# Decode attention and an MLP on one core: the projection's weights on every fourth partition, larger last pieces, and another order at the start

## Chip, cores and metric

One core of one Trainium2 chip runs the whole program in one launch. The metric is device time in microseconds; "median of the runs" is over separate timed runs without the profiler, and a profiled execution is one further run whose records are read here. The engines are PE (matrix multiply, with its weight loads listed as PEld), DVE (vector), ACT (scalar functions), POOL (general), and SP, which here only issues transfers. The transfers of SP's and ACT's queues run on 16 DMA engines.

## The reference, cut to what matters

```python
def _A_ref(x, k_cache, v_cache, wq, wo):          # B=2, Sq=1, D=1024, H=32, Sk=16384, Dh=128, bf16
    q = (x @ wq).reshape(B, Sq, H, Dh).transpose(0, 2, 1, 3)
    scores = einsum("bhqd,bhkd->bhqk", q, k_cache) * (Dh ** -0.5)
    p = softmax(scores)
    o = einsum("bhqk,bhkd->bhqd", p, v_cache)
    return o.transpose(0, 2, 1, 3).reshape(B, Sq, H * Dh) @ wo

def _B_ref(x, w1, w2, w3, w4):                    # F=3584
    h = gelu(layernorm(x) @ w1)
    hs = (quarters of h, shifted along S and padded with zeros) @ w2
    x1 = x + hs
    return x1 + gelu(layernorm(x1) @ w3) @ w4

g = sigmoid((x * gate_w).sum(-1))
out = g * A + (1 - g) * B
```

Each of the two caches is 2 x 32 x 16384 x 128 bf16 values, 256 MiB; K and V together are nearly all of the 572.53 MB that the program reads. With S = 1 every shifted quarter of h is zero, so the product with w2 is one with zeros; the kernel computes it with the zero tile `shT`.

## The kernel before, in words

**Units.** The attention is done in 32 units: 16 head pairs i, and in each the two batch rows s = 0 and 1. A unit's K is 8 MiB, held as 64 KB on each of the 128 partitions, and its V likewise. The buffer `mem` has five cells of 32 KB per partition. K of s = 0 lies in cells 0 and 1, K of s = 1 in cells 1 and 2, V in cells 3 and 4. As the two Ks share a cell, a K may be loaded once the unit before has transposed the first four of its eight chunks, those in the shared cell (semaphore `tr3`). A V may be loaded once the V before has been used (`pvd`).

**One unit in the loop** (L875 to L884). POOL spreads the queries (`pool_unit`, L610). DVE transposes K chunk by chunk into the two buffers `kt` (`dve_scores`, L631); PE multiplies each chunk, 8 matmuls (`pe_scores`, L654). DVE transposes the scores and takes the maximum m (L638, L640). `softmax` (L663): ACT makes Dm, a diagonal matrix of m; PE spreads it (R); ACT takes the exponent into `pt` with its sums. `pe_pv` (L711) multiplies the V of the unit *before by one head pair* with its `pt`, 64 matmuls into `oacc`, and `dve_pv_end` (L772) adds up the rows into `red`. PE then brings the result into rows (`ot`, L717), and DVE copies it as bf16 to `OT` (L782). After s = 1, `pe_project` (L727) multiplies OT with wo's 256 rows of that head pair and adds to `arow` in PSUM. `total` (L684) takes R's minimum as the exponent's bias `nb` on DVE, sums on PE and inverts on DVE. Each engine goes through its own instructions in order and waits on semaphores, so an order written in the source is the order on each engine.

**SP's queue** in the loop (L868 to L874): wait for `tr3`, load K; wait for `pvd`, load the V of the head pair before; for s = 0 also wait for `wod` (the last projection is done) and load wo: 512 KB as 128 partitions with two rows of 2 KB each, 4 KB in one run. All transfers of the loop are in this one queue, each waiting instruction in front of those after it.

**The start.** SP loads wq into cells 3 and 4, w1 and w2 into cell 2, the first K; then, as cells come free, w3, the second unit's K (L803), w4 (L817) and, in the loop's first iteration, its K (L869) and V. The MLP is done between the first two units: the first layer norm and w1, w2; then the first half of unit 0's chunks; the second layer norm; `x1row` = x + hs on the few rows that hold data (L805 to L813, four DVE operations on two partitions each); the second half; w3's product; unit 0's softmax and `total`; the transpose of w3's product into the scratch `tsc` (L823) and its GELU; unit 1's chunks, w4's product, its softmax and `total`; then `brow` = (x1 + h2)(1 - g), L841 to L856.

**The end.** The V of the last head pair: s = 0 whole into cells 0 and 1 (L894), s = 1 in nine pieces of 32 or 16 rows (a row is one 128-wide position of each partition; 32 of them are 8 KB). The first three pieces go through `pv_moving` as in the loop (L939), the others one row at a time straight into the last accumulation (L952), so that each is used as it lands. Then the last two heads' wo rows, in a tile of their own (`wo_l`), the last projection (L963), the sum with `brow` (L970) and the stores.

`Line` (L21) is a helper that derives waits from names read and written; `ln.wait` makes an engine wait for stamps.

Of the kernel before, what the change touches and what calls it, by code (L numbers as in the profile page):

```python
# [88 lines left out]
def kernel(  # L89
# [36 lines left out]
    FQ = F // Q4  # L126
    HQ = H // Q4
    assert NCK == 8 and NG <= QP and FC * QP == FQ and KC * QP == NQ

# [14 lines left out]
    kt = [sb([P, CT * Dh // 2], FP32, f"kt{k}") for k in range(2)]  # L144
    wo_t = sb([P, 2, D], BF16, "wo")
    wo_l = sb([P, 2, D], BF16, "wo_last")
    st = sb([P, GT, QP], FP32, "st")
    Dm = sb([P, P], FP32, "Dm")
    tsc = sb([P, HQ * Dh], FP32, "tsc")
    xin = sb([P, B, KC], BF16, "xin")  # L150
    xrow = sb([P, NQ], BF16, "xrow")
    gwT = sb([P, KC], BF16, "gwT")
# [22 lines left out]
    h2T = sb([P, FC, B], BF16, "h2T")  # L175
    x1row = sb([P, NQ], FP32, "x1row")
    brow = sb([P, NQ], FP32, "brow")
# [9 lines left out]
    part = sb([P, Dh], FP32, "part")  # L187
    red = sb([P, 2, Dh], FP32, "red")
    OT = sb([P, 2, B], BF16, "OT")
    OTl = sb([P, 2, B], BF16, "OT_last")  # L190
    out_row = sb([P, NQ], BF16, "out_row")

    sps = [psum.tile([P, GT * QP], FP32, name=f"S{k}") for k in range(2)]
# [15 lines left out]
    v_rows = A_v_cache.rearrange("b (g t) s d -> b g (t s d)", t=2)  # L209
    wo_rows = A_wo.rearrange("(g p r) n -> g (p r n)", p=P, r=2)  # L210

# [7 lines left out]
    def wo_source(hp):  # L219
        flat = wo_rows[hp : hp + 1, :] if isinstance(hp, int) else wo_rows[bass.ds(hp, 1), :]  # L220
        return flat.rearrange("o (p x) -> (o p) x", p=P)

# [13 lines left out]
    with tc.tile_critical(no_gpsimd_drain=True):  # L236
# [10 lines left out]
        ln.dma("ACT", xin[:], A_x.rearrange("b s (p r) -> p (b s) r", p=P), "l_x", writes=["xin"])  # L247
        ln.dma("ACT", gwT[:], gate_w.rearrange("(p r) -> p r", p=P), "l_gw", writes=["gwT"])
        for b in range(B):
            ln.dma(  # L250
                "ACT", xrow[b : b + QP * (Q4 - 1) + 1 : QP, :],
                A_x[b, 0].rearrange("(k n) -> k n", k=Q4), f"l_xr{b}", writes=[f"xrow{b}"],
            )
# [12 lines left out]
        for k in range(2):  # L266
            ln.op("POOL", lambda k=k: POOL.memset(pts[k][:], 0.0), writes=[f"pt{k}"])

        for k in range(2):
            ln.op("DVE", lambda k=k: DVE.memset(oacc[k], 0.0), writes=[f"oacc{k}"])  # L270
# [4 lines left out]
        ln.op("DVE", lambda: DVE.memset(shT[:], 0.0), writes=["shT"])  # L275
        ln.op("DVE", lambda: DVE.memset(brow[:], 0.0), writes=["brow"])
        ln.op("DVE", lambda: DVE.memset(hm2[:], 0.0), writes=["hm2"])
# [384 lines left out]

        def softmax(u):  # L663
            s = u.s
            wait(PE, "dm", u.after(1))
            PE.matmul(R_ps[:, 0:P], lhsT=ones_f[:], rhs=Dm[:], start=True, stop=True).then_inc(S("rr"), 1)  # L666
            wait(ACT, "mx", u.after(1))
            ACT.activation(out=Dm[:], in_=ident_s[:], func=ACTF.Copy, scale=m_t[:, 0:1]).then_inc(S("dm"), 1)  # L668
            wait(ACT, "nbd", u.after(1))
            if not u.first:  # L670
                wait(ACT, "pvd", u.after(0))
            for e in range(2):
                rows = slice(e * HALF, (e + 1) * HALF)
                ins = ACT.activation(  # L674
                    out=pts[s][rows, :, e, :].rearrange("p (m a) k -> p a k m", a=GT // 4),
                    in_=st[rows, :, 0:NG].rearrange("p (a k) m -> p a k m", k=4),
                    func=ACTF.Exp,
                    bias=nb_t[rows],
                    scale=scale,
                    accum_out=rs_t[rows],  # L680
                )
            ins.then_inc(S("ex"), 1)

        def total(u):  # L684
            s = u.s
            wait(DVE, "rr", u.after(1))
            for e in range(2):
                rows = slice(e * HALF, (e + 1) * HALF)
                ins = DVE.tensor_reduce(out=nb_t[rows], in_=R_ps[rows, rows], axis=AX.X, op=ALU.min)  # L689
            ins.then_inc(S("nbd"), 1)  # L690
            wait(PE, "ex", u.after(1))
            PE.matmul(tot_ps[:, 0:1], lhsT=lmat[:], rhs=rs_t[:], start=True, stop=True).then_inc(S("tt"), 1)  # L692
            wait(DVE, "tt", u.after(1))
            DVE.reciprocal(out=rinv[s][:], in_=tot_ps[:, 0:1]).then_inc(S("rcp"), 1)  # L694

# [15 lines left out]
        def pe_pv(u):  # L711
# [3 lines left out]
            wait(PE, "rd", u.after(-1))  # L715
            for r in range(2):
                ins = PE.matmul(  # L717
                    ot_ps[:, 2 * r : 2 * r + 2],
                    lhsT=red[:].rearrange("p e d -> p (e d)")[:, r : 2 * Dh : 2],
                    rhs=hsel[:],  # L720
                    start=True,
                    stop=True,
                    skip_group_check=True,
                )
            ins.then_inc(S("otd"), 1)

        def pe_project(u):  # L727
            wait(PE, "wol", u.v_landed)
            wait(PE, "OTd", u.after(-1))
            for r in range(2):  # L730
                for k in range(Q4):
# [40 lines left out]
        def dve_pv_end(u):  # L772
# [4 lines left out]
            dve_rows(s, maskr[s], u.after(-1)).then_inc(S("rd"), 1)  # L777
            wait(DVE, "otd", u.after(-1))
            wait(DVE, "wod", u.i)
            for e in range(2):  # L780
                rows = slice(e * HALF, (e + 1) * HALF)
                ins = DVE.tensor_copy(  # L782
                    out=OT[rows, :, s],
                    in_=ot_ps[rows, 0:4].rearrange("p (r e) -> p e r", e=2)[:, e],
                )
            ins.then_inc(S("OTd"), 1)

# [16 lines left out]
        layernorm_T(x1T[:], xn2T[:], "ln2", "x1T", "xn2T")  # L804
        for g in range(Q4):  # L805
            rows = slice(QP * g, QP * g + B)
            ln.op(
                "DVE",
                lambda rows=rows: DVE.tensor_tensor(  # L809
                    out=x1row[rows, :], in0=ot_ps[rows, :], in1=xrow[rows, :], op=ALU.add  # L810
                ),
                reads=["ot", "xrow0", "xrow1"], writes=["x1row"],
            )  # L813
        dve_scores(u0, NCK // 2)
# [3 lines left out]
        pe_scores(u0, NCK - 1)  # L818
        softmax(u0)
        total(u0)  # L820
        ln.op(
# [7 lines left out]
        gelu_T(columns(FC), h2T[:], FC, "g2", "h2T")  # L829

        pool_unit(u1)
        dve_scores(u1)
        pe_scores(u1, 0, NCK - 1)
        linear(h2T, w4_v, FC, D, "h2T", "c3", [ot_ps[:]], ["ot"])
        pe_scores(u1, NCK - 1)
        softmax(u1)
        total(u1)
        ln.wait("PE", [ln.writer["ot"]])
        PE.sem_inc(S("pvd"), 1)
        PE.sem_inc(S("wod"), 1)  # L840
        for g in range(Q4):  # L841
            rows = slice(QP * g, QP * g + B)
            ln.op(
                "DVE",
                lambda rows=rows: DVE.tensor_tensor(
                    out=brow[rows, :], in0=ot_ps[rows, :], in1=x1row[rows, :], op=ALU.add
                ),
                reads=["ot", "x1row"], writes=["brow"],
            )
        ln.op(  # L850
# [4 lines left out]
            reads=["brow", "omgrow"], writes=["brow"],  # L855
        )  # L856

        with nc.Fori(1, HP) as i:
# [5 lines left out]
            for s in range(2):  # L864
# [7 lines left out]
                if s == 0:  # L872
                    wait(SP, "wod", i)
                    SP.dma_start(out=wo_t[:].rearrange("p r n -> p (r n)"), in_=wo_source(i - 1)).then_inc(S("wol"), 16)  # L874
            for u in units:  # L875
                pool_unit(u)
                dve_scores(u)
                pe_scores(u)
                softmax(u)
                pe_pv(u)  # L880
                dve_pv_end(u)
                if u.s == 1:
                    pe_project(u)
                total(u)  # L884

        landed = [f"l_{x}" for x in ("wq", "w1", "w2", "x", "gw", "xr0", "xr1", "w3", "w4")]
        landed += [f"l_v31_{n}" for n in range(3)]

        def landing(n):
            return 32 if n < 9 else 16  # L890

        PIECES = [32] * 7 + [16] * 2
        wait(SP, "tr3", 2 * HP)
# [3 lines left out]
        for n, size in enumerate(PIECES):  # L897
# [4 lines left out]
            at += size  # L902
        wo_heads = A_wo.rearrange("(h d) n -> d h n", d=Dh)
        for e in range(2):
            SP.dma_start(out=wo_l[:, e, :], in_=wo_heads[:, H - 2 + e, :]).then_inc(S(landed[len(PIECES) + 1 + e]), 16)  # L905

# [32 lines left out]
        for n in range(3):  # L939
            wait(PE, landed[n + 1], landing(n + 1))  # L940
            ins = pv_moving(V, 1, n * 8, (n + 1) * 8, moving // 4)
        ins.then_inc(S("pvd"), 1)
# [66 lines left out]
```

## Time and profile before

| | us |
|---|---|
| runs | 1335.42, 1335.53, 1336.2; median 1335.53 |
| profiled execution: its time | 1336.33 |
| profiled execution: span, first to last instruction | 1334.6 |
| PE busy | 748.9 (56%), 4920 matmuls |
| DVE busy | 710.5 (53%), 712 instructions |
| ACT busy | 104.6 (8%) |
| POOL busy | 12.4 (1%) |
| mean granted PE clock | 0.808 |
| read from HBM | 572.53 MB, 429 GB/s over the span |
| transposes of K (L631) | 256 of 2.28 us, 570.7 |
| score matmuls (L654) | 2048, 548.9 |

The page divides the span into 40 slices and shows how busy each engine and the DMA engines were in them; it lists the costliest groups of instructions with what they waited for; and it follows the chain of work that ended last back through what released each step. For each issue of a transfer the trace has the time from issue to landing, when its semaphore is complete. A transfer's time to landing includes what was queued before it. An idle engine costs nothing while something else sets the end.

### The profile page before, as it was taken

How to read it: one execution, taken by the hardware profiler on the slowest of the kernel's cores; microseconds unless marked ns; L12 is line 12 of the kernel's file. 1: busy time of each engine (PE TensorE's matmuls, PEld its weight loads, DVE VectorE, ACT ScalarE, POOL GpSimd, SP SyncE). 2: the span in 40 equal slices, each digit the busy share in tenths (PEclk: the TensorE clock that was granted, in tenths of full speed). 3: DMA queues.
4: the chain of work that ended last, by engine and by line, in shares of the span. 5: the costliest groups of instructions: out<-in, count | busy, mean ns of one | idle time of the engine just before them, and what ended most of it. 6: DMA issues, size and time to landing. Idle time of an engine off the chain costs nothing.

```text
span 1334.6 us, 11800 instructions
## 1 busy us (share of the span) xinstructions
PE 748.9 (56%) x4920; PEld 302.2 (23%) x4920; DVE 710.5 (53%) x712; ACT 104.6 (8%) x164; POOL 12.4 (1%) x44
## 2 busy tenths in 40 slices
PE   0655666554566555466654546655455665555664
PEld 0222222222222222222222212222222222222222
DVE  1465565654556654456565445655444656545561
ACT  0010000000000000000000000000000000000000
POOL 0000000000000000000000000000000000000000
PEclk9778887777888777788777788877778877777886
DMA  9999999999999999999999999999999999999997
GB/s 409 437 419 425 431 433 432 430 438 430 434 432 434 432 432 438 426 438 430 434 432 434 436 428 438 428 436 431 434 438 428 436 428 438 424 441 436 430 436 317
DMA packets 13993, 572.68 MB, mean 429 GB/s; under 512 B 1936, under 2 KB 1952, under 8 KB 4384
## 3 DMA queue, kind: packets, MB, share of 16 engines
q1 hardware_dynamic: 13544, 572.53, 99.5%
q8 instruction: 8, 0.13, 0.0%
q10 hardware_dynamic: 440, 0.01, 0.0%
q14 instruction: 1, 0.01, 0.0%
HBM read 572.53 MB, written 0.00 MB: 429 GB/s over the span
## 4 chain that ended last, share of the span: by engine, by line
DMA 65%; DVE 16%; PE 12%; issue 5%; SPq 1%; POOL 0%; ACT 0%; POOLq 0%; ACTq 0%
DMA mem<-in_A_k_cache_dram 64%; DVE kt L631 15%; PE S L654 11%; DMA wo_last<-in_A_wo_dram 2%; SPq L898 1%; PE oacc L699 0%; PE oacc L510 0%; ACT pt L674 0%; SPq L905 0%; SPq L869 0%; DVE x1row L809 0%; DVE st L638 0%; POOL ln_rstd L450 0%; POOL qw L265 0%; DVE tsc L823 0%
## 5 line engine op out<-in xcount | busy, mean ns | idle before, releaser
L654 PE MATMUL S<-kt,qw 128*128 128x512 bf16 x2048 | 548.9, 418 | 306.8 <-DVE kt L631 306.7
L631 DVE STREAM_TRANSPOSE kt<-mem 128x2048 f32<-128x2048 f32 x256 | 570.7, 2283 | 208.0 <-DMA mem<-in_A_k_cache_dram 154.6
L654 PEld LDWEIGHTS S<-kt,qw 128*128 128x128 bf16 x2048 | 196.3, 104 | 645.7 <-issue 338.9
L699 PE MATMUL oacc<-mem,pt 128*8 128x512 bf16 x2008 | 115.9, 384 | 4.0 <-DMA mem<-in_A_v_cache_dram 4.0
L674 ACT ACTIVATE pt<-st,nb 64x256 bf16<-64x256 f32 x64 | 89.7, 1401 | 226.0 <-DVE nb L689 225.5
L747 DVE TENSOR_SCALAR part<-oacc,maskr 128x128 f32<-128x128 f32 x31 | 10.9, 351 | 143.0 <-PE oacc L699 143.0
L668 ACT ACTIVATE Dm<-ident_s,m 128x128 f32<-128x128 f32 x32 | 12.8, 401 | 921.2 <-DVE m L640 921.2
L692 PE MATMUL tot<-rs,lmat 128*128 128x1 f32 x64 | 18.7, 362 | 105.3 <-ACT pt L674 105.3
L694 DVE RECIPROCAL rinv<-tot 128x1 f32<-128x1 f32 x32 | 5.4, 168 | 113.1 <-PE tot L692 113.1
L699 PEld LDWEIGHTS oacc<-mem,pt 128*8 128x8 bf16 x2008 | 46.2, 87 | 61.3 <-DMA mem<-in_A_v_cache_dram 4.1
L638 DVE STREAM_TRANSPOSE st<-S 128x512 f32<-128x512 f32 x32 | 22.9, 717 | 69.8 <-PE S L654 69.8
L717 PE MATMUL ot<-hsel,red 128*128 128x2 f32 x120 | 19.0, 263 | 54.7 <-DVE red L753 54.7
L666 PE MATMUL R<-Dm,ones_f 128*128 128x128 f32 x64 | 15.6, 326 | 54.4 <-ACT Dm L668 54.4
L692 PEld LDWEIGHTS tot<-rs,lmat 128*128 128x128 f32 x64 | 16.0, 311 | 112.3 <-ACT pt L674 112.3
L717 PEld LDWEIGHTS ot<-hsel,red 128*128 128x128 f32 x120 | 16.4, 196 | 69.8 <-DVE red L753 69.8
L674 ACT ACTIVATION_READ_ACCUMULATOR pt<-st,nb 64x1 f32 x64 | 30.6, 478 | 0.0
L666 PEld LDWEIGHTS R<-Dm,ones_f 128*128 128x128 f32 x64 | 9.5, 188 | 70.2 <-ACT Dm L668 70.2
L753 DVE SCALAR_TENSOR_TENSOR part<-oacc,maskr,part 128x128 f32<-128x128 f32 x62 | 21.7, 351 | 2.2
L782 DVE CAST OT<-ot 64x2 bf16<-64x2 f32 x60 | 9.6, 160 | 22.2 <-PE ot L717 21.8
L344 PE MATMUL tot<-zp,ones_f 128*128 128x2 f32 x2 | 0.6, 364 | 33.7 <-DVE zp L366 33.7
L615 POOL TENSOR_TENSOR qw<-qd,mask 128x16 bf16<-128x16 f32 (+1 forms) x32 | 8.4, 263 | 1138.6 <-PE S L654 1138.6
L689 DVE TENSOR_REDUCE nb<-R 64x1 f32<-64x64 f32 x64 | 14.2, 222 | 3.4 <-PE R L666 2.1
(104 smaller groups left out, 116.0 us busy)
## 6 DMA issues: line engine op xcount, KB each, us to landing
mem<-in_B_w_dram SPq DMA_DIRECT2D x2, 7168.0 KB, 27.6
wo<-in_A_wo_dram SPq DMA_DIRECT2D x15, 512.0 KB, 28.5
mem<-in_A_v_cache_dram SPq DMA_DIRECT2D x7, 1024.0 KB, 18.4
mem<-in_B_w_dram SPq DMA_DIRECT2D x2, 2048.0 KB, 29.3
mem<-in_A_v_cache_dram SPq DMA_DIRECT2D x2, 512.0 KB, 27.7
mem<-in_A_k_cache_dram SPq DMA_DIRECT2D x32, 28.3
wo_last<-in_A_wo_dram SPq DMA_DIRECT2D x2, 256.0 KB, 21.6
mem<-in_A_v_cache_dram SPq DMA_DIRECT2D x31, 30.9
```

Of the source, the lines that this page charges most:

```text
L631: DVE.transpose(out=kt[n % 2][:], in_=k_view(s)[:, c * CT : (c + 1) * CT, :].rearrange("p j d -> p (j d)").bitcast(FP32),).then_inc(S(f"tr ...
L638: DVE.transpose(out=st[:].rearrange("p j r -> p (j r)"), in_=sps[s][:]).then_inc(S("stT"), 1)
L654: ins = PE.matmul(sps[s][:].rearrange("p (j k) -> p j k", k=QP), lhsT=qw[s][:, v, NG - 1 - m : NG - 1 - m + P], rhs=ktb[:, half * GT : (ha ...
L666: PE.matmul(R_ps[:, 0:P], lhsT=ones_f[:], rhs=Dm[:], start=True, stop=True).then_inc(S("rr"), 1)
L668: ACT.activation(out=Dm[:], in_=ident_s[:], func=ACTF.Copy, scale=m_t[:, 0:1]).then_inc(S("dm"), 1)
L674: ins = ACT.activation(out=pts[s][rows, :, e, :].rearrange("p (m a) k -> p a k m", a=GT // 4), in_=st[rows, :, 0:NG].rearrange("p (a k) m ...
L689: ins = DVE.tensor_reduce(out=nb_t[rows], in_=R_ps[rows, rows], axis=AX.X, op=ALU.min)
L692: PE.matmul(tot_ps[:, 0:1], lhsT=lmat[:], rhs=rs_t[:], start=True, stop=True).then_inc(S("tt"), 1)
L699: ins = PE.matmul(oacc[s][QP * q : QP * q + 8, :], lhsT=pts[s][:, g].rearrange("p h k -> p (h k)"), rhs=V[:, 4 * g : 4 * g + 4, :].rearran ...
L717: ins = PE.matmul(ot_ps[:, 2 * r : 2 * r + 2], lhsT=red[:].rearrange("p e d -> p (e d)")[:, r : 2 * Dh : 2], rhs=hsel[:], start=True, stop ...
L753: ins = DVE.scalar_tensor_tensor(out=red[:] if twice else part[:], in0=in0.unsqueeze(1).to_broadcast([P, 2, Dh]) if twice else in0, scalar ...
L898: SP.dma_start(out=region(V_CELL, NJ * Dh)[:, at * Dh : (at + size) * Dh], in_=unit_rows(v_rows, HP - 1, 1)[:, at * Dh : (at + size) * Dh] ...
```

## The change

**wo on 32 partitions.** The tile `wo` becomes 16 KB on each of 128 partitions. A head pair's 256 rows are loaded as 32 runs of 16 KB (8 rows each) to the partitions 0, 4, 8, ... 124; the other partitions hold zeros, written once at the start by POOL (two memsets). So PE goes over all 128 partitions as before, eight rows deep instead of two: `ot` is made by eight matmuls per unit in place of two (each is two PE instructions), from `red` with its columns shifted by r, and `arow` by 32 in place of 8. OT has eight columns; a `tensor_scalar` with one half's mask and a `scalar_tensor_tensor` with the other's replace the two copies. `red` gets eight zero columns behind it.

**Room for it.** `tsc` becomes a view of wo's first two rows (cleared by POOL after its last use, before wo is first loaded), `xrow` a name for `out_row`, `wo_last` a view of cell 2 (loaded after the last K is transposed), and `x1row` is gone. x + hs is now added into `brow` over all 128 partitions, one operation, so `xrow` is cleared first.

**The order at the start.** `softmax` and `total` are split into `spread_max`, `bias`, `exponent`, `total`, `invert`, called in the same order in the loop. At the start the GELU of w3's product comes straight behind `spread_max` of unit 0, ahead of its `bias` and `exponent`; unit 0's `total` and `invert` come after the first half of unit 1's transposes and before the second; `brow`'s first sum stands there too. The signal that frees the V cells is given straight after w4's product; the one that lets wo be loaded is given after `brow`.

**Last pieces.** 64, 64, 64, 32, 16, 16 rows in place of seven times 32 and two times 16; the first three still go through `pv_moving`, now 192 rows instead of 96.

```diff
+    WR = 8
+    WP = 2 * Dh // WR
+    WS = P // WP
...
-    wo_t = sb([P, 2, D], BF16, "wo")
-    wo_l = sb([P, 2, D], BF16, "wo_last")
+    wo_t = sb([P, WR, D], BF16, "wo")
+    wo_rest = wo_t[:, 2:WR, :].rearrange("p r n -> p (r n)").bitcast(FP32)
...
-    tsc = sb([P, HQ * Dh], FP32, "tsc")
+    tsc = wo_t[:, 0:2, :].rearrange("p r n -> p (r n)").bitcast(FP32)
     xin = sb([P, B, KC], BF16, "xin")
-    xrow = sb([P, NQ], BF16, "xrow")
...
-    x1row = sb([P, NQ], FP32, "x1row")
...
-    red = sb([P, 2, Dh], FP32, "red")
-    OT = sb([P, 2, B], BF16, "OT")
+    red_t = sb([P, 2 * Dh + WR], FP32, "red")
+    red = red_t[:, 0 : 2 * Dh].rearrange("p (e d) -> p e d", e=2)
+    oa = sb([P, WR], FP32, "oa")
+    OT = sb([P, WR, B], BF16, "OT")
...
     out_row = sb([P, NQ], BF16, "out_row")
+    xrow = out_row
...
-    wo_rows = A_wo.rearrange("(g p r) n -> g (p r n)", p=P, r=2)
+    wo_rows = A_wo.rearrange("(g p r) n -> g (p r n)", p=WP, r=WR)
...
-        return flat.rearrange("o (p x) -> (o p) x", p=P)
+        return flat.rearrange("o (p x) -> (o p) x", p=WP)
...
+        ln.op("DVE", lambda: DVE.memset(xrow[:], 0.0), writes=["xrow0", "xrow1"])
...
+        ln.op("POOL", lambda: POOL.memset(wo_rest, 0.0), writes=["wo"])
...
-        ln.op("DVE", lambda: DVE.memset(brow[:], 0.0), writes=["brow"])
+        ln.op("DVE", lambda: DVE.memset(red_t[:], 0.0), writes=["red"])
...
-        def softmax(u):
-            s = u.s
+        def spread_max(u):
+            wait(ACT, "mx", u.after(1))
+            ACT.activation(out=Dm[:], in_=ident_s[:], func=ACTF.Copy, scale=m_t[:, 0:1]).then_inc(S("dm"), 1)
             wait(PE, "dm", u.after(1))
             PE.matmul(R_ps[:, 0:P], lhsT=ones_f[:], rhs=Dm[:], start=True, stop=True).then_inc(S("rr"), 1)
-            wait(ACT, "mx", u.after(1))
-            ACT.activation(out=Dm[:], in_=ident_s[:], func=ACTF.Copy, scale=m_t[:, 0:1]).then_inc(S("dm"), 1)
+
+        def exponent(u):
+            s = u.s
             wait(ACT, "nbd", u.after(1))
             if not u.first:
                 wait(ACT, "pvd", u.after(0))
@@ -681,17 +690,20 @@
                 )
...
-        def total(u):
-            s = u.s
+        def bias(u):
             wait(DVE, "rr", u.after(1))
             for e in range(2):
                 rows = slice(e * HALF, (e + 1) * HALF)
                 ins = DVE.tensor_reduce(out=nb_t[rows], in_=R_ps[rows, rows], axis=AX.X, op=ALU.min)
             ins.then_inc(S("nbd"), 1)
+
+        def total(u):
             wait(PE, "ex", u.after(1))
             PE.matmul(tot_ps[:, 0:1], lhsT=lmat[:], rhs=rs_t[:], start=True, stop=True).then_inc(S("tt"), 1)
+
+        def invert(u):
             wait(DVE, "tt", u.after(1))
-            DVE.reciprocal(out=rinv[s][:], in_=tot_ps[:, 0:1]).then_inc(S("rcp"), 1)
+            DVE.reciprocal(out=rinv[u.s][:], in_=tot_ps[:, 0:1]).then_inc(S("rcp"), 1)
...
-            for r in range(2):
+            for r in range(WR):
                 ins = PE.matmul(
                     ot_ps[:, 2 * r : 2 * r + 2],
-                    lhsT=red[:].rearrange("p e d -> p (e d)")[:, r : 2 * Dh : 2],
+                    lhsT=red_t[:, r : r + 2 * P - 1 : 2],
...
-            for r in range(2):
+            for r in range(WR):
                 for k in range(Q4):
                     ins = PE.matmul(
                         arow[k],
...
+            ot = ot_ps[:, 0 : 2 * WR].rearrange("p (r e) -> p e r", e=2)
+            DVE.tensor_scalar(
+                out=oa[:], in0=ot[:, 0, :], scalar1=hm2[:, 0:1], scalar2=None, op0=ALU.mult
+            ).then_inc(S("oad"), 1)
+            wait(DVE, "oad", u.after(-1))
             wait(DVE, "wod", u.i)
-            for e in range(2):
-                rows = slice(e * HALF, (e + 1) * HALF)
-                ins = DVE.tensor_copy(
-                    out=OT[rows, :, s],
-                    in_=ot_ps[rows, 0:4].rearrange("p (r e) -> p e r", e=2)[:, e],
-                )
-            ins.then_inc(S("OTd"), 1)
+            DVE.scalar_tensor_tensor(
+                out=OT[:, :, s], in0=ot[:, 1, :], scalar=hm2[:, 1:2], in1=oa[:], op0=ALU.mult, op1=ALU.add
+            ).then_inc(S("OTd"), 1)
...
-        for g in range(Q4):
-            rows = slice(QP * g, QP * g + B)
-            ln.op(
-                "DVE",
-                lambda rows=rows: DVE.tensor_tensor(
-                    out=x1row[rows, :], in0=ot_ps[rows, :], in1=xrow[rows, :], op=ALU.add
-                ),
-                reads=["ot", "xrow0", "xrow1"], writes=["x1row"],
-            )
         dve_scores(u0, NCK // 2)
         pe_scores(u0, NCK // 2 - 1, NCK - 1)
         linear(xn2T, w3_v, KC, F, "xn2T", "c3", [oacc[0], oacc[1]], ["oacc0", "oacc1"])
         ln.dma("SP", region(3, FC * D), w_rows[3], "l_w4", writes=["c3"])
         pe_scores(u0, NCK - 1)
-        softmax(u0)
-        total(u0)
+        spread_max(u0)
...
         gelu_T(columns(FC), h2T[:], FC, "g2", "h2T")
-
+        bias(u0)
+        exponent(u0)
+        ln.op("POOL", lambda: POOL.memset(tsc[:], 0.0), writes=["tsc"])
         pool_unit(u1)
-        dve_scores(u1)
-        pe_scores(u1, 0, NCK - 1)
+        dve_scores(u1, 0, NCK // 2)
+        pe_scores(u1, 0, NCK // 2 - 1)
+        total(u0)
+        invert(u0)
+        ln.op(
+            "DVE", lambda: DVE.tensor_tensor(out=brow[:], in0=ot_ps[:], in1=xrow[:], op=ALU.add),
+            reads=["ot", "xrow0", "xrow1"], writes=["brow"],
+        )
+        dve_scores(u1, NCK // 2)
+        pe_scores(u1, NCK // 2 - 1, NCK - 1)
         linear(h2T, w4_v, FC, D, "h2T", "c3", [ot_ps[:]], ["ot"])
-        pe_scores(u1, NCK - 1)
-        softmax(u1)
-        total(u1)
         ln.wait("PE", [ln.writer["ot"]])
         PE.sem_inc(S("pvd"), 1)
-        PE.sem_inc(S("wod"), 1)
-        for g in range(Q4):
-            rows = slice(QP * g, QP * g + B)
-            ln.op(
-                "DVE",
-                lambda rows=rows: DVE.tensor_tensor(
-                    out=brow[rows, :], in0=ot_ps[rows, :], in1=x1row[rows, :], op=ALU.add
-                ),
-                reads=["ot", "x1row"], writes=["brow"],
-            )
+        pe_scores(u1, NCK - 1)
+        spread_max(u1)
+        bias(u1)
+        exponent(u1)
+        ln.op(
+            "DVE", lambda: DVE.tensor_tensor(out=brow[:], in0=ot_ps[:], in1=brow[:], op=ALU.add),
+            reads=["ot", "brow"], writes=["brow"],
+        )
+        total(u1)
+        invert(u1)
         ln.op(
             "DVE",
             lambda: DVE.tensor_scalar(
@@ -854,6 +864,9 @@
             ),
             reads=["brow", "omgrow"], writes=["brow"],
         )
+        ln.wait("PE", [ln.writer["brow"]])
+        ln.wait("SP", [ln.writer["tsc"], ln.writer["wo"]])
+        PE.sem_inc(S("wod"), 1)
...
-                    SP.dma_start(out=wo_t[:].rearrange("p r n -> p (r n)"), in_=wo_source(i - 1)).then_inc(S("wol"), 16)
+                    SP.dma_start(out=wo_t[0:P:WS].rearrange("p r n -> p (r n)"), in_=wo_source(i - 1)).then_inc(S("wol"), 16)
...
-                softmax(u)
+                spread_max(u)
                 pe_pv(u)
                 dve_pv_end(u)
                 if u.s == 1:
                     pe_project(u)
+                bias(u)
+                exponent(u)
                 total(u)
+                invert(u)
...
-        landed += [f"l_v31_{n}" for n in range(3)]
...
         def landing(n):
-            return 32 if n < 9 else 16
-
-        PIECES = [32] * 7 + [16] * 2
+            return 32
+
+        PIECES = [64, 64, 64, 32, 16, 16]
...
+        wo_l = region(2, 2 * D).rearrange("p (e n) -> p e n", e=2)
+        wait(SP, f"tr{NCK - 1}", 2 * HP)
         for e in range(2):
             SP.dma_start(out=wo_l[:, e, :], in_=wo_heads[:, H - 2 + e, :]).then_inc(S(landed[len(PIECES) + 1 + e]), 16)
...
-            ins = pv_moving(V, 1, n * 8, (n + 1) * 8, moving // 4)
+            ins = pv_moving(V, 1, n * 16, (n + 1) * 16, moving // 4)
```

## The prediction, made before the result was known

> **What bounds it now.** I read the page's busy slices and DMA queues first, because a kernel that streams two caches is likely to be a transfer with work beside it.
>
> ```profile
> DMA  9999999999999999999999999999999999999997
> GB/s 409 437 419 425 431 433 432 430 438 430 434 432 434 432 432 438 426 438 430 434 432 434 436 428 438 428 436 431 434 438 428 436 428 438 424 441 436 430 436 317
> ...
> q1 hardware_dynamic: 13544, 572.53, 99.5%
> ...
> DMA 65%; DVE 16%; PE 12%; issue 5%; SPq 1%; POOL 0%; ACT 0%; POOLq 0%; ACTq 0%
> ```
>
> SP's queue alone fills 99.5% of the 16 engines' span, and no slice between the first and the last falls below 419 GB/s. The chain's 16% DVE and 12% PE are pieces during which transfers ran on too, so only two things can move the end: fewer seconds of transfer for the same bytes, or a gap in the stream. Second I read the chain of waits in the steady loop.
>
> ```profile
> 679.45 2.32 DVE kt L631
> ...
> 690.11 29.31 DMA mem<-in_A_k_cache_dram
> 719.44 2.32 DVE kt L631
> ...
> 730.20 27.93 DMA mem<-in_A_k_cache_dram
> 758.15 2.32 DVE kt L631
> ```
>
> Each transpose after a wait starts as its K lands: 679.45, 719.44, 758.15. From K1 to the next K0 two 8 MiB loads pass in 758.15 - 719.44 = 38.71 us (19.36 each, 2.42 per MiB); from K0 to K1 the same two and wo pass in 719.44 - 679.45 = 39.99, in other iterations 39.98. So **wo costs 1.27 us** where its 512 KB at the cache's rate would be 1.21: its 4 KB rows carry a surcharge of 0.06. Third, the slack on the engines in a unit that projects:
>
> ```profile
> 669.66 0.63 PE L717 MATMUL ot<-hsel,red 128*128 128x2 f32 x4 [1.82 <-DVE red L753]
> 670.33 0.33 DVE L782 CAST OT<-ot 64x2 bf16<-64x2 f32 x2 [0.72 <-PE ot L717]
> ...
> 670.81 0.39 PE L732 MATMUL arow<-wo,OT 128*2 128x256 bf16 x8 [0.52 <-DVE OT L782]
> ...
> 671.38 0.33 SPq L874 DMA_DIRECT2D wo<-in_A_wo_dram  x1
> ...
> 679.45 4.51 DVE L631 STREAM_TRANSPOSE kt<-mem 128x2048 f32<-128x2048 f32 x2 [4.60 <-DMA mem<-in_A_k_cache_dram]
> ```
>
> DVE idles 4.60 us before K lands (5.99 in the other unit). Fourth, I looked for a gap in the start, issue by issue, with each issue's time to landing:
>
> ```profile
> 82.09 0.33 SPq L82 DMA_DIRECT2D mem<-in_B_w_dram  x1
> ...
> 92.93 4.50 DVE L631 STREAM_TRANSPOSE kt<-mem 128x2048 f32<-128x2048 f32 x2
> ...
> 103.33 0.35 SPq L869 DMA_DIRECT2D mem<-in_A_k_cache_dram  x1
> ```
>
> ```profile
> mem<-in_B_w_dram SPq DMA_DIRECT2D x1, 7168.0 KB, 25.1
> ...
> mem<-in_A_k_cache_dram SPq DMA_DIRECT2D x1, 25.1
> ```
>
> (the second view's last column: us to landing, for the issues at 82.09 and 103.33). w4 landed at 82.09 + 25.1 = 107.2; the next K, issued 3.9 us before that, at 103.33 + 25.1 = 128.4 (DVE starts on it at 128.48). That is 21.3 us for a load of 19.36: **a gap of 1.9 us**, the only one I find. Unit 1's K, issued at 63.77 and landed 26.5 later at 90.3, had a lead of 7.2 us on w3's landing (40.84 + 30.1 = 70.9) and took 19.4: no gap. So 3.9 us of lead is too little and 7.2 is enough.
>
> **The change, part by part.** *Start.* K0 of iteration 1 is issued when unit 1's fourth transpose is done, 103.33 - 92.93 = 10.40 us after its first. That first one stood behind the GELU, which stood behind unit 0's exponent (86.62 to 89.45) and `tot`. In the new order the GELU needs only m and w3's product, and the exponent runs on ACT beside DVE. m ends at 85.05, and 1.8 us earlier (83.3) because the four `x1row` adds (66.98 to 68.76) are gone from in front. From the old tsc transpose to the old first kt was 90.21 to 92.93, 2.7 us; with nb's 0.46 DVE is free near 86.5. Then it waits for unit 1's K, at 90.3. So the first transpose moves from 92.93 to 90.3 and no further; K0's issue from 103.33 to 100.7, a lead of 6.5 us on w4. `rinv`, `brow` (0.17 + 0.42 us) come behind the fourth transpose and delay K0 by nothing. The bounds are 0 (6.5 is still too little) and 1.9 + 0.16, since the next interval, 128.48 to 168.62, is 40.14 against 39.98 later. 6.5 lies near the 7.2 that left no gap: I take **-2.0 us**. V0 of iteration 1 goes out after w4's product, near 113 instead of 122.52: its stream is full anyway.
>
> New waits there: SP waits for POOL's clear of `tsc` before K0. A POOL memset of 128x512 bf16 takes 0.526 us; 1024 floats are between 1.05 (by elements) and 2.1 (by bytes), from about 85 on, so done by 87 with SP next wanted at 100.7. `qw` of unit 1 is queued behind it, 0.26 more, wanted at 92.6. The clear of 3072 floats at the start (3.2 to 6.3 us) ends by 10, and POOL is wanted at 45.84. ACT's two xrow loads wait for one DVE memset near 0.3 us; their data is read after 60. All nothing.
>
> *Loop.* ot: 16 PE instructions for 4; the four take 0.63, 0.14 for each further: +1.7 us. OT: two DVE operations on 128x8 for two copies of 0.16; by the nearest rows (0.23 for 128x2 at L921, 0.35 for 128x128 at L753) +0.2. `arow`: 32 for 8, at most 4 x 0.39, +1.2, beside the exponent. DVE ends 1.9 us later per unit, inside its 4.60: nothing. wo's issue moves from 671.38 to about 674.5; V is issued before it, and behind it on SP stands only K1, which waits until 690.11 anyway. If the cover were gone, K would be late by the excess, and behind that is K0's lead of 758.15 - 19.36 - 730.20 = 8.6 us.
>
> wo's load: a quarter of the rows, each 16 KB. No row shows a load of this size to 32 partitions. Best, the surcharge goes wholly, -0.06 x 15 = -0.9. Worst, it goes by partitions, 32 of 128: 4 x 1.27 = 5.1 us, +3.8 x 15 = +57. The bytes, their contiguous source and the even four-apart spread are those of a full load, so I take it near the best row: a quarter of the surcharge stays, **-0.7 us**. [...]
>
> *End.* The last V's rows: one MiB in 8 KB rows landed in 2.49 us against 2.42.
>
> ```profile
> 1323.98 1.01 PE L952 MATMUL R<-pt,mem 128*128 128x2 bf16 x32 [1.53 <-DMA mem<-in_A_v_cache_dram]
> 1326.48 1.01 PE L952 MATMUL R<-pt,mem 128*128 128x2 bf16 x32 [1.48 <-DMA mem<-in_A_v_cache_dram]
> ...
> 1330.26 0.09 PEld L963 LDWEIGHTS arow<-wo_last,OT_last 128*2 128x2 bf16 x4 [0.34 <-DMA wo_last<-in_A_wo_dram]
> ```
>
> Six of seven such MiB get 16 KB rows: 0.07 x 6 is saved by half or whole, 0.2 to 0.4, **-0.3**. But the third piece now ends at row 192, 64 rows before the last, so it lands near 1328.98 - 2 x 2.49 = 1324.0. Behind it come 16 matmuls (24 took 1.47 at 1316.87; at the halved clock of that stretch up to 1.9), DVE's rows and L947 (from 1318.34 to 1320.47: 2.1), 32 and 16 matmuls (1.0 + 0.6): 1328.7 to 1329.6, and the last piece waits from 1328.98. So OT is 0 to 0.6 late, of which wo_last's own wait covers 0.3: **+0.2**. wo_last's wait for the last transpose is over near 1289, before its turn.
>
> Sum: -2.0 - 0.7 - 0.3 + 0.2 = **-2.8 us**. The profiled execution took 1336.33 (span 1334.6 and 1.7 around it): 1333.5. It is 0.8 above the median of the runs, 1335.53, on which scale the forecast is **1332.7 us**.
>
> **Rivals.** *The 32-partition load collides (slower).* Place: each of 15 wo loads. If several DMA engines at a time write to the same part of SBUF, they halve each other: 2.54 for 1.27 us, +1.27 x 15 = +19, without the -0.7: 1335.5 - 2.1 + 19 = 1352. For it: the stream has no slack, so each such microsecond counts; against: nothing in this trace. Even a part decides: from +0.14 us a load the rest of the gain (2.1) is gone. Full or partial, 1336 to 1352. [...]
>
> *The start keeps its gap.* If 6.5 us of lead does not do, or the slow first packets come anyway, only -0.8 is left: 1334.7. For it: 6.5 is below the one lead known to suffice. Against: half the missing lead or more is given.
>
> *The end or the loop eats it.* PE's last stretch at half clock, OT 0.6 late and more: 1333.5 at most; loop units would need over 4.60 us more, which the sum of 1.9 denies.
>
> **How the numbers follow.** My forecast has 0.58, with 1331.9 to 1333.6 as its own range; the gap that stays 0.12; the end that eats it 0.06; the collision 0.24, spread over 1336 to 1352. What a measurement of this kernel can tell from no change is about 0.2%, or 2.7 us: below 1332.9 is faster. The forecast sits on that edge, so I split it, 0.40 faster and 0.18 within; with the two small cases within, 0.36; the collision slower, 0.24, nearly all past 1338.2. The range reaches from 1331.7 to 1339, leaving out most of the collision and, as less likely still, the +57.
>
> **What would show it.** K0 of iteration 1 issued near 100.7 and landing 19.4 us after w4; the K0-to-K1 intervals at 39.92 to 39.94 and the others at 38.71 (the collision: 40.3 and more, and wo's packets a quarter as many); DVE's idle before K at 2.5 to 4; last V's third piece at 1324 less the shift, and wo_last still last to land. I am wrong if the K0-to-K1 interval grows, or if DVE no longer waits for K.

## The result, and the profile after

The changed kernel takes **1333.03 us** (median of 18 runs, 1332.67 to 1333.93) against 1335.86 for the kernel before in the same number of runs beside it (1334.77 to 1337.02): 2.8 us less, a ratio of 0.998 with a 95% interval of 0.9972 to 0.9987. The profiled execution took 1333.24 us, its span is 1331.2.

The page of the changed kernel, its busy slices and its main queue:

```profile
DMA  9999999999999999999999999999999999999997
GB/s 410 433 425 435 440 426 437 431 431 435 431 435 431 435 433 435 431 435 433 433 433 433 437 429 437 429 437 428 439 427 439 427 439 427 437 429 437 431 437 333
DMA packets 12120, 572.67 MB, mean 430 GB/s; under 512 B 1888, under 2 KB 1904, under 8 KB 2416
...
q1 hardware_dynamic: 11672, 572.53, 99.5%
```

The stream still fills the span and moves the same bytes, in 11672 packets instead of 13544: 15 loads of wo with 96 rows fewer each (1440), three issues of 128 rows fewer for the last V (384), and the other 48 are small ones. The chain of waits in the same stretch of the loop (start, duration, what):

```profile
638.07 2.32 DVE kt L638
...
649.54 27.19 DMA mem<-in_A_k_cache_dram
676.76 2.32 DVE kt L638
...
687.68 29.00 DMA mem<-in_A_k_cache_dram
716.69 2.33 DVE kt L638
```

From K1 to K0 it is 676.76 - 638.07 = 38.69, as before; from K0 to K1 716.69 - 676.76 = 39.93 where it was 39.98 or 39.99. The timeline of the projecting unit in that stretch (in brackets the idle time ahead of an instruction and what ended it):

```profile
667.67 2.06 PE L729 MATMUL ot<-hsel,red 128*128 128x2 f32 x16 [1.82 <-DVE red L765]
669.78 0.23 DVE L792 TENSOR_SCALAR oa<-ot,hm 128x8 f32<-128x8 f32 x1 [2.16 <-PE ot L729]
...
670.41 1.88 PE L744 MATMUL arow<-wo,OT 128*2 128x256 bf16 x32 [0.68 <-DVE OT L797]
...
672.47 0.50 SPq L887 DMA_DIRECT2D wo<-in_A_wo_dram  x1
...
676.76 4.50 DVE L638 STREAM_TRANSPOSE kt<-mem 128x2048 f32<-128x2048 f32 x2 [2.42 <-DMA mem<-in_A_k_cache_dram]
```

The work on wo grew (`ot` from 0.63 to 2.06 us, `arow` from 0.39 to 1.88), and DVE still idles 2.42 us before K lands, 4.60 before the change. The start, first the timeline and then the issues with their time to landing (last column) at 78.86 and 100.71:

```profile
89.89 4.50 DVE L638 STREAM_TRANSPOSE kt<-mem 128x2048 f32<-128x2048 f32 x2 [4.39 <-DMA mem<-in_A_k_cache_dram]
...
100.71 0.35 SPq L882 DMA_DIRECT2D mem<-in_A_k_cache_dram  x1
```

```profile
mem<-in_B_w_dram SPq DMA_DIRECT2D x1, 7168.0 KB, 27.9
...
mem<-in_A_k_cache_dram SPq DMA_DIRECT2D x1, 25.4
```

Unit 1's first transpose now waits for its K alone. w4 lands at 106.8 and the next K at 126.1, 19.3 us later: the gap is closed. The end, in the chain of waits:

```profile
1295.30 25.13 DMA mem<-in_A_v_cache_dram
1320.47 1.91 PE oacc L711 x16
...
1324.68 1.72 PE R L969 x64
1326.42 0.17 DVE OT_last L975
1326.64 0.63 PE arow L980 x8
1327.29 0.42 DVE out_row L987
```

Behind the third piece PE no longer waits for any transfer: its 64 matmuls run in one piece, and what ends last is PE's and DVE's work, where before it was the landing of the last weights. These landed at 1326.7; `out_row` began 0.60 us later, before the change 0.43.

Where the 3.4 us between the two profiled spans come from can be read off at three places. The chain has the K of iteration 1 and the last K, in the kernel before and in the changed one:

```profile
128.48 2.32 DVE kt L631
...
1270.33 2.32 DVE kt L631
```

```profile
126.18 2.32 DVE kt L638
...
1267.08 2.32 DVE kt L638
```

The K of iteration 1 lands at 126.18 and not 128.48: -2.30. From there to the last K's landing (1267.08, before 1270.33) it is 1140.90 us and not 1141.85: -0.95, or 0.063 for each of 15 loads of wo. From there to the last weights' landing 59.6 and not 59.9: -0.3, and to `out_row` 0.17 more.

### The profile page after: what moved, and what is told of

It is laid out like the page before. It is cut to its first block, busy times and chain, and to the rows that moved or that the text cites. A ratio compares the mean times of both kernels' runs of the same rounds, so it can differ in the third digit from the quotient of the medians.

```text
span 1331.2 us, 13091 instructions
## 1 busy us (share of the span) xinstructions
PE 822.5 (62%) x5568; PEld 362.8 (27%) x5568; DVE 712.7 (54%) x707; ACT 104.9 (8%) x164; POOL 15.9 (1%) x46
## 3 DMA queue, kind: packets, MB, share of 16 engines
q1 hardware_dynamic: 11672, 572.53, 99.5%
## 4 chain that ended last, share of the span: by engine, by line
DMA 67%; DVE 14%; PE 13%; issue 4%; POOL 0%; SPq 0%; another core or an unknown queue 0%; ACT 0%; POOLq 0%
DMA mem<-in_A_k_cache_dram 66%; DVE kt L638 14%; PE S L661 12%; DMA mem<-in_A_v_cache_dram 2%; PE oacc L711 0%; PE ot L517 0%; POOL wo L274 0%; SPq L882 0%; PE R L969 0%; POOL qw L270 0%; POOL pt L272 0%; SPq L913 0%; DVE st L645 0%; DVE part L765 0%
## 5 line engine op out<-in xcount | busy, mean ns | idle before, releaser
L711 PE MATMUL oacc<-mem,pt 128*8 128x512 bf16 x2032 | 118.6, 386 | 6.7 <-DMA mem<-in_A_v_cache_dram 6.7
L729 PE MATMUL ot<-hsel,red 128*128 128x2 f32 x480 | 68.3, 273 | 54.7 <-DVE red L765 54.7
L729 PEld LDWEIGHTS ot<-hsel,red 128*128 128x128 f32 x480 | 65.8, 215 | 69.8 <-DVE red L765 69.8
L702 PE MATMUL tot<-rs,lmat 128*128 128x1 f32 x64 | 18.4, 357 | 79.5 <-ACT pt L683 79.5
L792 DVE TENSOR_SCALAR oa<-ot,hm 128x8 f32<-128x8 f32 x30 | 6.8, 225 | 71.1 <-PE ot L729 71.1
L744 PE MATMUL arow<-wo,OT 128*2 128x256 bf16 x480 | 28.1, 413 | 10.1 <-DVE OT L797 10.1
```

The lines of the kernel that those rows point to most:

```text
L711: ins = PE.matmul(oacc[s][QP * q : QP * q + 8, :], lhsT=pts[s][:, g].rearrange("p h k -> p (h k)"), rhs=V[:, 4 * g : 4 * g + 4, :].rearran ...
L729: ins = PE.matmul(ot_ps[:, 2 * r : 2 * r + 2], lhsT=red_t[:, r : r + 2 * P - 1 : 2], rhs=hsel[:], start=True, stop=True, skip_group_check= ...
L744: ins = PE.matmul(arow[k], lhsT=OT[:, r, :], rhs=wo_t[:, r, k * NQ : (k + 1) * NQ], start=False, stop=False, skip_group_check=True,)
```

## The experiments

Each kernel ran beside the kernel before on one chip. Two changed kernels that did not run side by side are compared by their landings, and not by their medians, where they differ by less than about 0.5 us.

**The start alone**, on the kernel before: its diff is that of the order at the start, without the clear of `tsc` and SP's wait for it.

> The kernel before with the new order at the start alone (softmax and total split, GELU ahead of unit 0's exponent, x + hs summed in brow, the signal for V straight after w4's product); wo stays in 4 KB runs on 128 partitions and the last V in nine pieces. If the start's gain is the gap ahead of iteration 1's K0, that K is issued near 100.7 and lands near 126.2 us (128.48 before), the K0-to-K1 intervals stay at 39.98, the last K lands 2.0 to 2.3 us earlier than 1270.33, and the time falls by 2.0 to 2.3. The rival, that the smaller packets of wo or of the pieces make the start's difference as well, or that the gain at the start is given back later, expects less than 1 us.

Measured: 1333.89 us against 1335.54, ratio 0.9988 (0.9979 to 0.9997), -1.65. K0 was issued at 100.95 and landed at 126.45, the K0-to-K1 intervals are 39.97 to 39.99, and the last K landed at 1268.0, 2.3 earlier than in the profile before. The start's gain is there by itself, and it is kept to the end. The runs give 0.6 less than the two profiles: the profiled execution before, 1336.33, was on the slow side of its own runs.

**The start taken back**, on the changed kernel:

```diff
-        spread_max(u0)
+        spread_max(u0); bias(u0); exponent(u0); total(u0); invert(u0)
 ... tsc, gelu_T
-        bias(u0)
-        exponent(u0)
 ... clear of tsc, pool_unit(u1)
-        dve_scores(u1, 0, NCK // 2) ... total(u0), invert(u0), brow ... dve_scores(u1, NCK // 2)
+        dve_scores(u1)
```

> The changed kernel with the order at the start taken back (unit 0's exponent and total ahead of the GELU, four x1row adds on few partitions, the V signal after unit 1's total). If the three parts add up, K0 of iteration 1 lands near 128.4 again, the K0-to-K1 intervals stay at 39.93, and the time stands 2.0 to 2.3 us above the changed kernel and 0.8 to 1.2 below the kernel before. If the parts depend on one another, it stands within 1 us of the changed kernel.

Measured: 1335.40 against 1335.54, ratio 0.9998 (0.9989 to 1.0007), so 2.4 above the changed kernel but not the 0.8 to 1.2 below the kernel before. The loop's part is there (39.93). What was lost is in the start: K0 went out at 104.78, 1.4 us later than in the kernel before, and landed at 129.1. In this mixed order the clear of `tsc` on POOL stands beside the GELU and in front of unit 1's transposes: one GELU step on DVE took 0.77 us in place of 0.19, and the first transpose began 0.5 later than in the kernel before (93.42 against 92.93). PE then took longer over the first 16 score matmuls, 6.38 us from 95.88 on against 4.95 from 95.39 on in the kernel before. The changed kernel has the long GELU step too, but there it costs nothing, since the first transpose waits for its K. The parts add up only as long as none of them moves K0.

**K0 issued one transpose later**, on the changed kernel:

```diff
+        wait(SP, "tr4", 2)
         with nc.Fori(1, HP) as i:
```

> The changed kernel with iteration 1's K0 issued one transpose later, near 103.7 and not 100.71; all else stays. If the lead on w4's landing (106.8) is what makes the gap, a lead of 3.1 us leaves one of 2 us or a little more: K0 lands near 128.5, the time is up by 2 to 3. If 3 us of lead are enough and the earlier gap had another cause in the old order, nothing.

Measured: 1334.80, ratio 0.9991 (0.9981 to 1.0001); 1.8 us above the changed kernel, a little less than the 2 to 3 expected. The issue in the timeline:

```profile
104.02 0.36 SPq L884 DMA_DIRECT2D mem<-in_A_k_cache_dram  x1
```

It landed 23.9 us after, at 127.9, 21.0 after w4. The edit moves nothing else (the V behind it still went out at 113.07), so the lead is the cause. Put together, with w4's landing and K0's from the six traces:

| kernel | K0 issued | lead on w4's landing | K0 lands after w4 by |
|---|---|---|---|
| start taken back | 104.78 | 2.0 | 22.3 |
| K0 one transpose later | 104.02 | 2.9 | 21.0 |
| before | 103.33 | 3.9 | 21.2 |
| shorter third piece (below) | 101.52 | 5.4 | 19.5 |
| changed | 100.71 | 6.1 | 19.3 |
| start alone | 100.95 | 6.2 | 19.3 |

A load of 8 MiB takes 19.36 in the loop. A lead of 5.4 us leaves no gap, 3.9 leaves almost 2 us; where it turns between them was not tried, and why 3.9 us are not enough the traces do not show. In two other traces of variants of the changed kernel, wo in 4 KB runs and the old pieces, the lead is 6.2 and 6.1, and K0 lands 19.3 and 19.6 after w4. The runs show a second sign: without the gap they lie close (changed 1332.67 to 1333.93, start alone 1333.69 to 1334.13), with it they spread over 2 us and more (before 1334.77 to 1337.02, start taken back 1333.64 to 1336.51, this one 1333.50 to 1335.61). This fits a gap that costs a different amount in each run; where it lies is seen in one trace of each kernel only.

**wo in runs of 4 KB**, on the changed kernel:

```diff
-                    SP.dma_start(out=wo_t[0:P:WS]..., in_=wo_source(i - 1)).then_inc(S("wol"), 16)
+                    for k in range(4):
+                        part4 = slice(k * 2 * D, (k + 1) * 2 * D)
+                        SP.dma_start(out=wo_t[0:P:WS]...[:, part4], in_=wo_source(i - 1)[:, part4]).then_inc(S(f"wol{k}"), 16)
```

> The changed kernel with wo on the same 32 partitions four apart, but loaded in four transfers with runs of 4 KB each (as many packets as before the change). If the loop's gain is the surcharge per packet, the K0-to-K1 interval goes back to 39.98 or 40.0 (39.93 in the changed kernel, 38.70 for the others), +0.8 to +1.2 us in all. If the gain is from the place on 32 partitions, it stays at 39.93.

Measured: 1333.84, ratio 0.9986 (0.9976 to 0.9995), 0.8 above the changed kernel; the K0-to-K1 intervals are 39.98 to 40.0. On the same partitions, the shorter runs bring back the whole surcharge of 0.06 us a load: it belongs to the length of the run, not to the place. (The load is four issues here in place of one; the kernel before has the same interval with one issue and as many rows.)

**wo in a block of 32 partitions, and on every second one**, on the changed kernel (`wo_t[0:WP]`, `wo_t[0 : 2 * WP : 2]` as the target; PE's work is the same, but on the wrong rows):

> The changed kernel with wo's 32 runs of 16 KB written to partitions 0 to 31 and not to every fourth one; PE's work is the same, but it multiplies with the wrong rows. If where the runs are written matters (several DMA engines at the same part of SBUF, the rival in which the load collides), the K0-to-K1 interval grows from 39.93 to 40.5 or up to 41.2, +9 to +19 us in all. If only the length of a run matters, the interval stays at 39.93.

> The changed kernel with wo's 32 runs of 16 KB on every second one of the first 64 partitions; PE multiplies with the wrong rows. If 32 partitions in a block collide because they lie close together, two apart halves what the block cost: K0-to-K1 near 42 (39.93 four apart, 43.8 in a block). If it is the lower half of the partitions as such that is slow, it stays near 43.8; if only neighbours of four share a way in, it is back at 39.93 to 40.5.

Measured: 1391.49 (four runs, 1380.87 to 1402.39), ratio 1.038 (1.0331 to 1.0428), for the block; 1397.06 in a single execution for every second one. Chain of the block:

```profile
704.36 2.32 DVE kt L638
...
715.17 32.82 DMA mem<-in_A_k_cache_dram
748.01 2.32 DVE kt L638
```

K0 to K1 is 748.01 - 704.36 = 43.65 us here, 43.8 on average, 3.9 more than four apart, while the other intervals stay at 38.70. Two apart is no better, 43.1 to 45.5. So the place matters, as the rival said: where the runs are written can cost each load 3.9 us. Neither nearness nor row length is what decides, since the rows are as long in all three, and a block and every second one cost about the same. Both lie in the lower 64 partitions, while four apart spreads over all 128. Whether that half as such is slow was not tried, and why a load there costs the stream 5.1 us (43.8 - 38.70) and not 1.2 the traces do not show.

**ot made twice**, on the changed kernel (`for r in [*range(WR)] * 2`):

> The changed kernel with each unit's eight ot matmuls done twice, +2.06 us in every unit's chain behind PV. DVE idles 2.42 and 4.17 us before the two K landings of an iteration, 6.6 together, and the two units would take 4.1 of them: if the cover holds, DVE's idle is down to about 0.4 and 2.1 and the time stays within 0.3 us. If the loop were already set by the units' chain, +2 us per unit, 60 in all, and 30 if only the projecting unit's.

Measured: 1342.37, ratio 1.0052 (1.0035 to 1.0068), 9.3 above the changed kernel; my expectation fell. The timeline of one unit, and three of its windows (PE busy, PEld, DVE, ACT, POOL, granted clock, DMA share, GB/s):

```profile
512.82 6.32 PE L729 MATMUL ot<-hsel,red 128*128 128x2 f32 x32 [1.82 <-DVE red L765]
519.18 0.23 DVE L792 TENSOR_SCALAR oa<-ot,hm 128x8 f32<-128x8 f32 x1 [6.42 <-PE ot L729]
...
524.69 2.31 DVE L638 STREAM_TRANSPOSE kt<-mem 128x2048 f32<-128x2048 f32 x1 [0.94 <-issue]
```

```profile
512.00:513.00 1.00, 0.18 (x2) 0.18 (x2) 0.73 (x2) 0.00 (x0) 0.00 (x0) 1.00 1.21 524
513.00:514.00 1.00, 1.00 (x9) 1.00 (x9) 0.00 (x0) 0.00 (x0) 0.00 (x0) 0.84 0.76 328
514.00:515.00 1.00, 1.00 (x7) 1.00 (x6) 0.00 (x0) 0.00 (x0) 0.00 (x0) 0.50 1.36 590
```

The 32 instructions took 6.32 us here, not 4.12: PV's wide matmuls ended at 511.0, the granted clock was 1.00 until 513, 0.84 in the next us and 0.50 from 514 on, and the later ones took longer (one took 352 ns in the median of all units, 258 in the changed kernel). In the 28 units that the chain of waits lists the doubled `ot` took 4.92 to 6.53; over all 30, by DVE's wait for it, 5.72 on average; the changed kernel's took 2.06 in 19 units and up to 3.17 in the others, on average 2.28. That is 3.4 us more per unit, 6.9 per iteration, and the cover is 6.6 (2.42 + 4.17). From the second iteration on DVE waits for no landing, and the loop is set by the chain through PE and DVE. An excess of 0.3 per iteration makes 4 us in 15; the two profiled executions lie 7.1 apart and the medians 9.3, so a part of the loss is not accounted for. In the unit of the changed kernel shown above, `ot` ended at 669.73, and the granted clock was 1.00 up to 670 and 0.64 in the next us. So the cover holds for the changed kernel, but it is small: less than 3.3 us per unit on average.

**The old pieces, and a shorter third piece**, on the changed kernel (`[32] * 7 + [16] * 2`; `[64, 64, 32, 32, 32, 16, 16]`):

> The changed kernel with the last V in nine pieces of 32 and 16 rows again. By the sum: from the last K's landing to the last weights' landing 59.9 us again (59.6 in the changed kernel), and the chain at the end waits for those weights and not for PE; the two nearly cancel, so the end of out_row comes 0.1 to 0.2 us later than in the changed kernel, no difference that the runs can tell. The rival, that larger pieces matter by fewer issues on SP, expects 1 us or more.

> The changed kernel with pieces of 64, 64, 32, 32, 32, 16, 16 rows, so that the last rows that go through oacc are the 160th and not the 192nd. If PE's work behind the third piece is what ends last, it now starts 2.4 us earlier, the chain's end is the landing of the last weights again, and out_row ends 0.43 us behind that landing and not 0.6; the smaller runs cost 0.04 to 0.07. Gain 0.1 us, at most 0.2: a look at the chain, not at the runs. If the end is set by the transfers already, nothing but the 0.04 to 0.07 of loss.

Measured: 1333.09 (0.9982, 0.9973 to 0.9991) and 1332.94 (0.9982, 0.9973 to 0.9991); neither can be told from the changed kernel. With the old pieces `out_row` comes at 1327.45, 0.16 later than in the changed kernel, and waits for the last weights again. With the shorter third piece that wait is back too, and `out_row` is at 1327.37: the expected gain of 0.1 is not there. The pieces are worth nothing that the runs show.

**Without w1 and w2**, on the changed kernel (their loads, the first layer norm, both products and the first GELU taken out, x1 copied from x), and the same with x and gate_w issued on SP ahead of wq; and that order alone as a control:

> The changed kernel without w1 and w2: with one position every shifted quarter of h is zero, so x1 is x for any finite w2, and the first layer norm, both products and the first GELU go too; the result stays the reference's. If the time is the stream of transfers and its gaps, 4 MiB fewer at 2.42 us per MiB are 9.7 us: 1323.3, or up to 2 us more where w3, issued once the product with wq is done, has less than 5 us of lead on the first K's landing. If PE, DVE or a fixed start set the time, less than half of that.

> As without w1 and w2, but x and gate_w are issued on SP ahead of wq and not on ACT beside it. In the run without w1 and w2, x (issued at 0.93) landed at 42.6, behind the first K's rows, so that the product with wq ended at 49.6 and w3 was issued 7 us after the stream had run dry. If that is where the 9.7 us went, x lands within 5 us now, w3 is issued near 30, and the time falls by 8.5 to 9.7 us against the changed kernel: 1323.3 to 1324.5. If the 4 MiB were never worth 9.7, it stays near 1332.

> The changed kernel with w1 and w2 as they are, and x and gate_w issued on SP ahead of wq: the control for the run above. w3's issue moves from 40 to about 30, but the stream had work there until 53: no gain. wq's issue comes two issues later, 0.9 us: 1333.0 to 1333.9.

Measured: 1332.70, ratio 0.9979 (0.9969 to 0.9989): 4 MiB fewer and nothing gained on the changed kernel, where 1323.3 to 1325.3 was expected. The timeline says where it went, and the issues how late x was:

```profile
42.56 0.17 DVE L354 COPY xT<-xin 128x16 bf16<-128x16 bf16 x1 [34.24 <-DMA xin<-in_A_x_dram]
...
49.74 0.33 SPq L82 DMA_DIRECT2D mem<-in_B_w_dram  x1
```

```profile
xin<-in_A_x_dram ACTq DMA_DIRECT2D x1, 4.0 KB, 41.6
...
mem<-in_A_k_cache_dram SPq DMA_DIRECT2D x1, 41.3
```

x, 4 KB, landed only with the end of the 16 MiB beside it, so the product with wq came late and w3 was issued 7 us after the first K had landed (1.43 + 41.3 = 42.7). With x ahead on the same queue:

```profile
xin<-in_A_x_dram SPq DMA_DIRECT2D x1, 4.0 KB, 1.8
```

w3 went out at 30.29, and the time is **1324.16** us (four runs, 1324.04 to 1324.29), ratio 0.9913 (0.9896 to 0.9929): 8.9 below the changed kernel, the 9.7 of the bytes less 0.9 for wq's two issues of delay. The control, with w1 and w2, takes 1334.09 (0.9988, 0.9978 to 0.9997): the early x by itself costs 1 us (its last K lands at 1268.06, in the changed kernel at 1267.08). So a gap again ate the whole of a saving, in another place, and closing it gave the saving back. This last kernel is the fastest here. It leaves out products that only meet zeros as long as there is one position, w2 is finite and the shift pads with zeros.

## Why the prediction was right

1332.7 was forecast and 1333.03 measured; -2.8 us from 1335.53 was forecast, and -2.8 from the 1335.86 of the runs beside it was measured. That the two agree to 0.1 us is in part luck: added up from the runs of the parts it is -1.65 (start), -0.8 (wo) and nothing (pieces), -2.45 together, and between the two profiled spans it is -3.4.

*The start, -2.0.* Right in its steps: first transpose at 90.3 (89.89), K0 issued at 100.7 (100.71), and a lead of 6.5 that was taken to be enough (6.1, and 5.4 was). The size is 2.3 between the two profiles, of which 0.4 was w4's own earlier landing, and 1.65 in the runs of the start alone. The 0.16 that the next interval was to give back came with the start alone (39.99) and not in the changed kernel (40.11 against 39.93 later). I read the gap from one execution; the spread of the runs fits a gap that differs from run to run. And by the same reckoning it was not the only one: w3's 7 MiB, worth 16.9 us, landed 18.4 behind the first K (52.56 to 70.94) in spite of 11.7 us of lead. In the changed kernel this is 16.9 (53.67 to 70.52), but w3 landed only 0.4 earlier: there it is the first K's landing that moved. An interval between two landings shows a gap only where the later landings move with it, as they did behind K0.

*wo, -0.7.* The mechanism was right, a surcharge on short runs: 39.98 to 40.0 between the landings with 4 KB, 39.93 with 16 KB. The term was a little small: the whole 0.06 went, 0.95 in the landings, 0.8 in the runs. That 32 runs four apart load as freely as 128 rows was my estimate, which no run had shown when it was made; the 39.93 shows it for this load. The worst end, +57, was worked out by partitions; the block of 32 came to +58. That shows the width of the bounds was not idle, and not that the rule by partitions holds: four apart has as many partitions and costs nothing. The agreement in size is luck.

*The loop's work, nothing.* `ot` +1.4 in most units and +1.65 on average (forecast 1.7), `arow` +1.5 (1.2), DVE's idle 2.42 and 4.17 (2.5 to 4). The claim behind it, that K0's lead of 8.6 us would cover what DVE's idle doesn't, was wrong for a lasting excess: a lead is used up once, and the doubled `ot` then paid in each iteration.

*The pieces, -0.3 + 0.2.* -0.3 and +0.17 in the traces, together nothing in the runs. The third piece landed at 1320.47, and PE took 1.91 us for its 16 matmuls at a granted clock of 0.50, as was priced.

*The rivals.* "The start keeps its gap": denied by the landing at 126.18; that a load's first packets are slow, no run shows. "The end eats it": the end is now PE's, at 0.17 us. "The load collides": not four apart (39.93). In a block the load is slowed (43.8), by what is not shown. That DMA engines at the same part of SBUF halve each other was my assumption, and no run shows it; I had put the price at +19 by it, and it is +58.

## What to carry to other kernels

In a kernel that is one stream of transfers, count the lead of each issue on the landing before it: here 5.4 us was enough and 3.9 was not, and a saved megabyte is worth nothing until the next issue is early enough to use it. Longer runs made fewer packets (11672 for 13544), which was worth 0.06 us per load of 512 KB here, and 32 partitions were enough for them where they lay four apart over all 128; in the lower 64 the same runs cost 3.9 us more a load in a block and 4.2 on every second one. Before adding work that is "hidden", add up what the cover is over a whole iteration, and at which clock the work will run.

## What the runs showed of the hardware

- A load of 512 KB in 32 runs of 16 KB cost the stream 1.2 us to partitions four apart, 5.1 to the lower 32 and 5.5 to every second one of the lower 64 (39.93, 43.8 and 44.2 between two landings, 38.70 without the load). Why is not shown.
- x, 4 KB in pieces of 16 bytes, took 27.0 us to land when it was issued on ACT's queue beside rows of 16 and 64 KB on SP's (the changed kernel), 41.6 beside rows of 64 KB alone (without w1 and w2), and 1.8 when it was issued ahead of those on SP's queue. Why is not shown.
- In the changed kernel's timeline the GELU step that took 0.19 us before takes 0.77 with a POOL memset beside it:

```profile
83.12 0.95 POOL L835 MEMSET wo<- 128x1024 f32 x1 [16.27 <-DVE g_pre L475]
83.35 0.77 DVE L482 TENSOR_SCALAR g_gsq<-g_gsq 128x56 f32<-128x56 f32 x1
```

The step ended at 84.12 and the memset at 84.07; in the kernel before, which has no memset there, the step at 91.82 took 0.19. That the one held up the other is not shown by more than these times.
